# Windowed attention and an MLP-mixer on one core: two opening channel products cut in halves, and the opening's loads and operations in another written order

## The chip, the cores and the metric

The kernel runs on one core of one Trainium2 chip. The metric is device time in microseconds for one execution. The engines named below are TensorE (PE in the profile), VectorE (DVE), ScalarE (ACT), GpSimd (POOL) and SyncE (SP, used here only to issue transfers).

## The reference

Inputs are q, k, v of shape 4 batches x 8 heads x 768 positions x 64, and four mixer weights. Per batch and head, attention is kept to the first 4 keys (the sinks) and to the last 128 keys of each query:

```
scores = scale * np.matmul(q, k.transpose(0, 1, 3, 2))
keep = is_sink | in_window            # key < 4, or 0 <= query - key < 128
a = softmax(np.where(keep, scores, -1e9))
x = (a @ v), heads side by side       # 768 x 512 for each batch
h = np.maximum(xt @ w_tok1, 0.0) @ w_tok2      # xt: x with positions last
u = x + h.transpose(0, 2, 1)
out = u + np.maximum(u @ w_ch1, 0.0) @ w_ch2   # 512 -> 1536 -> 512
```

## The kernel before

**Tiling.** The 32 heads are taken in 8 groups of 4; a batch is two groups (0 and 1, then 2 and 3, and so on). q and k of a group are loaded, cast to bf16 and turned by 32 x 32 blocks on DVE. Scores are made with keys on the partitions, so their exponential is already the transposed operand of the product with v. Key blocks are handled in three pairs (0, 1, 2). The mixer of a batch follows its two groups; its channel part takes the 768 positions in two halves of 384.

**Operations by name.** The kernel builds a list of small operations and names each:

- `Lq0.1` loads piece 1 of q of group 0 (L359 on SP for groups 0 and 1, L371 on POOL for later ones), `Lv` loads v (L381, SP), `Cq`, `Ck`, `Cv` cast, `Tq`, `Tk` turn (L403, DVE), `KZ` prepares the sink keys (L427, DVE).
- `SC0.12` is the score product of group 0, key pair 1, heads from 2 on (L448 and L455). In groups 0 and 1 it covers two heads and one bank, later four heads and two banks. `EX` is its exponential (L472, ACT), `MK` the mask multiplication in SBUF (L483, DVE), `SK` and `EXK` the same for the sinks (L509 PE, L514 ACT).
- `PV0.3` is the product with v for query block 3 of group 0 (L528, L531, L536), `XB0.3` its division by the row sum into `x_b` (L551, L552, DVE).
- `T1b.` is the first token product of batch b (L580), `H1b.` its rectifier; `TT` and `UE` make the transposed `uT` directly for the first half of batch 0, one pair for each of four channel blocks (L611 and L614 on PE; the evacuation at L233 or L235); `T2` and `U` make u in the other layout (L632 PE, L637 DVE), `X` and `UTE` transpose it (L642 PE; L233 or L235).
- `C10.03` is the first channel product of batch 0, half 0, block 3 of twelve (L665): four matmuls, one for each channel block of `uT`. `V` is its rectifier (L239 ACT or L241 DVE). `C20.200` is a third of the second channel product of batch 0, position block 2 (L687), `O` adds u (L697, DVE), `ST` stores (L702, SP).

**Order.** `order_of` is a planner: with an estimated duration for each operation it places, one after the other, the operation that can start first, choosing among those that start within 0.2 us by priority. Its result fixes the order of the instructions on every engine; each engine then runs its own list in that order and waits where a producer is late. For the opening the list `FIRST` gives each named operation its priority and its engine (`:P` is PE, `:A` ACT, `:D` DVE, `:G` POOL, `:S` SP). Everything that is not in `FIRST` is placed by the estimates, so it depends on the times which the planner expects for what stands ahead. `Filler` puts matmuls on zeros (`warm`, L800) where the planner expects PE to be idle in the first 29 us, at the start above all.

**PSUM.** Eight banks: two pairs called "sc" for scores (and for the paired `PV` of group 1) and four single banks called "mx" for everything else. A bank is taken by the first matmul of an operation and given back by the operation that reads it out (`XB` for a `PV`, `V` for a C1, `O` for a whole C2, `UTE` for an `X`). The planner also writes down which bank each operation takes.

**Staging.** The stage pool has four buffers for loaded v (and q, k of group 1). `behind_of` makes the load of `w_tok1` wait for v of group 0, and loads of v of groups 2 and 3 for the last part of `w_ch1`. In the emission order both before and after, `Lv0.0` stands ahead of `Lv1.0` and `Lv1.1`.

Of the kernel before, what the change touches and what calls it, by code (L numbers as in the profile page):

```python
# [9 lines left out]
FP32 = mybir.dt.float32  # L10
# [6 lines left out]


FIRST = """
warm:D blk:G Lq0.0:S kz:D vsink:A Lk0.0:S ones:D va:G Lq0.1:S zero:D first:G Lk0.1:S Lq1.0:S mneg:G first1:D  # L20
Lk1.0:S Lv0.0:S Lv1.0:S rest:G mnegs:D Cq0.0:A Lv1.1:S ident:G Tq0.0:D vs1:G Ck0.0:A vsl:G Tk0.0:D Cq0.1:A
Tq0.1:D Ck0.1:A Tk0.1:D KZ0:D SC0.22:P Cq1.0:G SC0.10:P EX0.21:A SC0.02:P EX0.10:A Tq1.0:D Ck1.0:G EX0.01:A
SC0.00:P SC0.12:P Tk1.0:D EX0.00:A SK0:P EX0.11:A Wtok1:G SC0.20:P Cv0:D EX0.20:A SC1.02:P Wtok2:G EXK0:A
SC1.10:P MK0.20:D Wch1.0:G EX1.01:A PV0.1:P PV0.3:P XB0.1:D Wch1.1:G PV0.5:P EX1.10:A KZ1:D SC1.20:P XB0.5:D
Wch1.2:G XB0.3:D SC1.00:P EX1.20:A Cv1:G PV0.0:P PV0.2:P XB0.0:D EX1.00:A SC1.12:P XB0.2:D Wch1.3:G SK1:P
EX1.11:A MK1.0256:D SC1.22:P Wch2.0:G MK1.00:D EXK1:A T10.000:P MK1.10:D Wch2.1:G PV1.0:P EX1.21:A PV1.1:P
T10.010:P PV0.4:P XB1.0:D PV1.2:P PV1.3:P XB0.4:D PV1.4:P XB1.2:D PV1.5:P T10.004:P XB1.4:D T10.014:P H10.00:A
T10.100:P H10.01:A T10.110:P T10.104:P T10.114:P H10.10:D TT0.00:P H10.11:A TT0.01:P UE0.00:A TT0.03:P
UE0.01:A TT0.02:P UE0.03:A UE0.02:A C10.03:P C10.02:P V0.03:A C10.00:P V0.02:A C10.01:P V0.00:A V0.01:D
"""  # L30


# [125 lines left out]
def kernel(  # L158
# [13 lines left out]
    nc = tc.nc  # L172
    B, H, S, D = q.shape
    P = 128
# [4 lines left out]
    NC = DM // P  # L179
# [5 lines left out]
    HS = S // 2  # L185
# [141 lines left out]
    groups = [Group() for _ in range(NG)]  # L327
# [236 lines left out]
    def mixer(b, base, mbase):  # L564
        M = batches[b]
# [4 lines left out]
        for a in range(GB):  # L570
            for tt in range(NTOK):
                p = Psum("mx", 1)

                xs, o, cut = groups[GB * b + a].xb, None, [0, 4, 6] if b == 0 else [0, 6]
                for lo, hi in zip(cut, cut[1:]):
                    def tok1(e, a=a, tt=tt, p=p, lo=lo, hi=hi):
                        if lo == 0:
                            open_psum(p, [P, W], FP32, "ps_h")
                        for t in range(lo, hi):
                            nc.tensor.matmul(p.tile, w_tok1[:, t, ts(tt, P)], xb.tile[:, t, ds(a * W, W)],  # L580
                                             start=(t == 0), stop=(t == NT - 1))
                    o = op(f"T1{b}.{a}{tt}{lo}", ("PE", 0.11 * (hi - lo)), tok1,
                           xs[:hi * len(xs) // NT] + [w_ops["tok1"], o], base, take=[p] if lo == 0 else [])
# [19 lines left out]
        if direct:  # L603
            for hf in range(NDIR):
                for c in range(NC):
                    p = Psum("mx", 1)
# [10 lines left out]
                    def evac(e, hf=hf, c=c, p=p):  # L617
                        copy_on[e](uT_of(hf)[:, c], p.tile)
                    a = c * P // W
                    o = op(f"TT{b}.{hf}{c}", ("PE", 0.5), tok2t,  # L620
                           M.h1[NTOK * a:NTOK * a + NTOK] + groups[GB * b + a].xb + [w_ops["tok2"]], base + 1 if hf == 0 else mbase + 0.2, take=[p])
# [4 lines left out]
        for st in range(NT):  # L626
            p, p2 = Psum("mx", 1), Psum("mx", 1)
# [19 lines left out]
            o = op(f"T2{b}.{st}", ("PE", 0.431), tok2, M.h1 + [w_ops["tok2"]], later, take=[p])  # L647
# [11 lines left out]
        def c1(hf, ft, pri):  # L659
            p = Psum("mx", 1)  # L660

            def emit(e):
                ps = open_psum(p, [P, HS], FP32, "ps_v")
                for c in range(NC):
                    nc.tensor.matmul(ps, w_ch1[:, c, ts(ft, P)], M.uT[hf][:, c], start=(c == 0), stop=(c == NC - 1))  # L665
            o = op(f"C1{b}.{hf}{ft}", ("PE", 0.652), emit,
                   M.ready[hf] + [w_ops["ch1", ft // 3]], pri, take=[p])
            M.c1.append(o)

            def relu(e):  # L670
                if M.v1t[hf] is None:
                    M.v1t[hf] = vpool.tile([P, NF, HS], BF16, name=f"v1{hf}")
                relu_on(e, M.v1t[hf][:, ft], p.tile)
            old = prev.c2[hf] if prev else []
            M.v1[hf].append(op(f"V{b}.{hf}{ft}", {"ACT": act(HS), "DVE": dve(HS)}, relu, [o] + old, pri - 5, free=[p]))
# [43 lines left out]
    w_ops = {}  # L719
# [29 lines left out]
        w_ops[key].follows = list(w_ops.values())[-2:-1]  # L749
        return w_ops[key]  # L750

    spq = [o for g in (0, 1) for o in groups[g].plain] + groups[0].load["v"] + groups[1].load["v"]
    for x, y in zip(spq, spq[1:]):
        y.follows = y.follows + [x]

    weight("tok1", w_tok1, moe_w_tok1.rearrange("(t p) n -> p t n", p=P), [groups[0].load["v"][0]], -40, 60)
    weight("tok2", w_tok2, moe_w_tok2.rearrange("(t p) n -> p t n", p=P), [], -39, 135)
    qf = DCH // 4
# [10 lines left out]
    for b in range(B):  # L769
        batches[b].x = X(batches[b - 2].u if b >= 2 else [])  # L770
        for a in range(GB):
            g = GB * b + a
# [9 lines left out]
    for n, word in enumerate(FIRST.split()):  # L782
        name, e = word.split(":")
        e = {"P": "PE", "A": "ACT", "D": "DVE", "G": "POOL", "S": "SP"}[e]
        o = by_name[name]
# [53 lines left out]
```

The softmax here doesn't subtract the row's maximum and nothing guards it: scores larger than these inputs give would overflow.

## Time and profile before

| | us |
|---|---|
| median of 6 runs | 215.89 (215.64 to 216.06) |
| the profiled execution, its own time | 215.94 |
| its span in the trace | 214.2 |
| PE busy | 205.3 (96%) |
| DVE busy | 126.4 (59%) |
| ACT busy | 108.2 (50%) |
| first score matmul starts | 11.16 |
| first channel matmul (L665) starts | 31.38 |

The time of an execution is 1.74 us more than the span: that part lies outside the first and last instruction. Matmuls overlap in their pipeline, so PE counts as busy also where it only just keeps up; a share of 96% over the span says nothing of one stage. The granted TensorE clock is full in all forty slices. The DMA engines are busy for nine tenths or more of the slices from about 5 to 75 us.

### The profile page before, as it was taken

How to read it: one execution, taken by the hardware profiler on the slowest of the kernel's cores; microseconds unless marked ns; L12 is line 12 of the kernel's file. 1: busy time of each engine (PE TensorE's matmuls, PEld its weight loads, DVE VectorE, ACT ScalarE, POOL GpSimd, SP SyncE). 2: the span in 40 equal slices, each digit the busy share in tenths (PEclk: the TensorE clock that was granted, in tenths of full speed). 3: DMA queues.
4: the chain of work that ended last, by engine and by line, in shares of the span. 5: the costliest groups of instructions: out<-in, count | busy, mean ns of one | idle time of the engine just before them, and what ended most of it. 6: DMA issues, size and time to landing. Idle time of an engine off the chain costs nothing.

```text
span 214.2 us, 4175 instructions
## 1 busy us (share of the span) xinstructions
PE 205.3 (96%) x1764; PEld 116.2 (54%) x1764; DVE 126.4 (59%) x224; ACT 108.2 (50%) x178; POOL 33.2 (15%) x54
## 2 busy tenths in 40 slices
PE   7999999999689999989999999999999999999993
PEld 2435776554356655466655544667555545655552
DVE  4786941598799989898998812786621122001121
ACT  7478556533847133989518520796553302743300
POOL 7739710002352200110000000000000000000000
PEclk9999999999999999999999999999999999999999
DMA  6999999999999982950001012100001122001122
GB/s 201 381 223 164 203 205 204 206 212 232 219 222 238 250 189 79 180 92 0 3 0 52 0 68 110 71 0 3 0 3 49 49 98 98 3 2 49 49 101 99
DMA packets 36244, 24.68 MB, mean 115 GB/s; under 512 B 26112, under 2 KB 30976, under 8 KB 36224
## 3 DMA queue, kind: packets, MB, share of 16 engines
q1 hardware_dynamic: 29184, 15.73, 28.8%
q0 software_dynamic: 7040, 8.67, 24.1%
q8 instruction: 14, 0.23, 0.4%
q14 instruction: 6, 0.05, 0.1%
HBM read 26.77 MB, written 6.29 MB: 154 GB/s over the span
## 4 chain that ended last, share of the span: by engine, by line
PE 91%; DVE 4%; ACT 2%; issue 1%; ACTq 0%
PE ps_w L687 29%; PE ps_v L665 28%; PE ps_s L455 7%; PE ps_h L580 5%; PE ps_warm L800 5%; PE ps_u L632 5%; PE ps_o L531 3%; DVE pT L483 2%; PE ps_o L528 2%; PE ps_o L536 2%; PE ps_ut L642 2%; ACT pT L472 2%; PE ps_k L509 1%; PE ps_s L448 1%; DVE x_b L552 1%
## 5 line engine op out<-in xcount | busy, mean ns | idle before, releaser
L665 PE MATMUL ps_v<-uT,w_ch 128*128 128x384 bf16 x384 | 67.9, 326 | 0.0
L239 ACT ACTIVATE v<-ps_v 128x384 bf16<-128x384 f32 x89 | 43.4, 493 | 48.5 <-PE ps_v L665 37.4
L687 PE MATMUL ps_w<-w_ch,v 128*128 128x512 bf16 (+1 forms) x300 | 66.1, 371 | 0.0
L472 ACT ACTIVATE pT<-ps_s 128x1024 bf16<-128x1024 f32 (+1 forms) x48 | 43.7, 954 | 13.9 <-PE ps_s L455 10.1
L665 PEld LDWEIGHTS <-w_ch 128*128 128x128 bf16 x384 | 36.5, 98 | 25.3 <-DVE x_b L552 0.4
L697 DVE TENSOR_TENSOR o<-ps_w,u_sb 128x512 f32<-128x512 f32 (+1 forms) x25 | 16.7, 669 | 55.9 <-PE ps_w L687 55.8
L687 PEld LDWEIGHTS <-v 128*128 128x128 bf16 x300 | 28.9, 98 | 29.6 <-issue 0.2
L483 DVE TENSOR_TENSOR pT<-pT,mrest 128x1536 bf16<-128x1536 bf16 (+2 forms) x21 | 20.8, 990 | 2.6 <-ACT pT L472 2.5
L637 DVE TENSOR_TENSOR u_sb<-ps_u,x_b 128x512 bf16<-128x512 f32 x24 | 15.2, 683 | 10.1 <-PE ps_u L632 10.1
L552 DVE TENSOR_TENSOR x_b<-ps_o,rc 128x256 bf16<-128x256 f32 (+1 forms) x45 | 19.9, 442 | 1.6
L455 PE MATMUL ps_s<-qT,kT 32*128 32x256 bf16 (+1 forms) x384 | 18.2, 263 | 1.0 <-ACT pT L472 1.0
L403 DVE STREAM_TRANSPOSE qT<-qb 128x768 uint32<-128x768 uint32 (+1 forms) x9 | 16.8, 1867 | 2.7 <-POOL qb L234 1.4
L531 PE MATMUL ps_o<-va,pT 128*128 128x65 bf16 x192 | 16.2, 194 | 1.0 <-DVE o L697 0.8
L403 DVE STREAM_TRANSPOSE kT<-kb 128x768 uint32<-128x768 uint32 (+1 forms) x9 | 16.9, 1874 | 0.4 <-POOL kb L234 0.4
L234 POOL CAST va<-raw_v 128x1536 bf16<-128x1536 f32 x7 | 10.3, 1477 | 41.6 <-DMA raw_v<-in_v_dram 24.5
L455 PEld LDWEIGHTS <-kT 32*128 32x128 bf16 x384 | 9.8, 92 | 11.2 <-issue 9.0
L531 PEld LDWEIGHTS <-pT 128*128 128x128 bf16 x192 | 13.5, 98 | 2.7 <-DVE o L697 1.2
L536 PE MATMUL ps_o<-va,pT 128*128 128x65 bf16 x160 | 14.8, 193 | 0.0
L632 PE MATMUL ps_u<-h,w_tok 128*128 128x512 bf16 x48 | 12.6, 378 | 0.6 <-ACT uT L235 0.5
L580 PE MATMUL ps_h<-x_b,w_tok 128*128 128x256 bf16 x96 | 12.2, 273 | 0.0
L800 PE MATMUL ps_warm<-warm 128*128 128x512 bf16 (+1 forms) x36 | 10.7, 464 | 1.3 <-DVE warm L255 1.3
L536 PEld LDWEIGHTS <-pT 128*128 128x128 bf16 x160 | 11.3, 98 | 0.8 <-issue 0.3
(63 smaller groups left out, 135.3 us busy)
## 6 DMA issues: line engine op xcount, KB each, us to landing
out_dram<-o SPq DMA_DIRECT2D x23, 256.0 KB, 2.0
raw_v<-in_v_dram SPq DMA_DIRECT2D x7, 768.0 KB, 12.3
qb<-in_q_dram POOLq DMA_DIRECT2D x6, 384.0 KB, 8.5
kb<-in_k_dram POOLq DMA_DIRECT2D x6, 384.0 KB, 12.4
w_ch<-in_moe_w_ch_dram POOLq DMA_DIRECT2D x4, 384.0 KB, 9.9
w_ch<-in_moe_w_ch_dram POOLq DMA_DIRECT2D x1, 1024.0 KB, 15.2
raw_q<-in_q_dram SPq DMA_DIRECT2D x2, 384.0 KB, 4.3
raw_k<-in_k_dram SPq DMA_DIRECT2D x2, 384.0 KB, 4.8
```

The lines of the kernel that those rows point to most:

```text
L239: nc.scalar.activation(o, i, AF.Relu)
L403: nc.vector.transpose(G.T[w].rearrange("p s x -> p (s x)").bitcast(UINT32).rearrange("p (i r) -> p r i", i=Q)[:, r], G.bf[w][:, r].bitcast ...
L455: nc.tensor.matmul(bank[h][:, at:at + w], G.T["k"][r, ts(kt, P), db], G.T["q"][r, ds(kt * P, w), db], start=not pem and db == 0, stop=db = ...
L472: nc.scalar.activation(o, i, AF.Exp, scale=scale)
L483: nc.vector.tensor_tensor(out=t, in0=t, op=ALU.mult, in1=m[:, 0:hi - lo].rearrange("p (o x) -> p o x", o=1).to_broadcast([P, GH, hi - lo]))
L531: nc.tensor.matmul(ps[:, h], G.pT[qt // 2][:, h, ds(256 * (qt % 2), P)], G.va[:, h, qt], start=(qt < 2 and h == 0), stop=(h == GH - 1 and ...
L536: nc.tensor.matmul(ps[:, h], G.pT[kt // 2][:, h, ds(256 * (kt % 2) + P, P)], G.va[:, h, kt], start=False, stop=(h == GH - 1), skip_group_c ...
L552: nc.vector.tensor_tensor(out=xb.tile[:, ds(q0, n), c0:c0 + W].rearrange("p n (h d) -> p n h d", h=GH), in0=ps[:, :, :, 0:D], in1=rc.to_br ...
L580: nc.tensor.matmul(p.tile, w_tok1[:, t, ts(tt, P)], xb.tile[:, t, ds(a * W, W)], start=(t == 0), stop=(t == NT - 1))
L632: nc.tensor.matmul(ps, w_tok2[:, tt, ts(st, P)], M.h1t[:, tt], start=(tt == 0), stop=(tt == NTOK - 1))
L665: nc.tensor.matmul(ps, w_ch1[:, c, ts(ft, P)], M.uT[hf][:, c], start=(c == 0), stop=(c == NC - 1))
L687: nc.tensor.matmul(p.tile, M.v1t[hf][:, ft, ts(st % NH, P)], w_ch2[:, ft, ds(lo, n)], start=(ft == 0), stop=(ft == NF - 1))
```

## The change

Three edits are made.

1. `FIRST` is rewritten. On SP the four quarter loads of group 0 come in the order k1, q1, q0, k0 in place of q0, k0, q1, k1. The cast of that first k piece goes from ACT to DVE, the cast of q of group 1 from POOL to DVE. On POOL the mask constants are built in another order (`blk` later). On PE the twelve score products of groups 0 and 1, and with them exponentials, masks and products with v, are listed in another order; `T20.3` and `T20.4`, which ran ahead of the first channel products because the planner placed them there, are no longer there; `UE0.02`, `V0.02` and `V0.00` go to DVE.
2. In `c1`, the first four blocks of half 0 of batch 0 are two operations each of two matmuls: `C10.00a` on channel blocks 0 and 1, `C10.00` on 2 and 3. Each half waits only for its own two blocks of `uT`; the second half adds into the same bank.
3. The planner's extra rule that placed the loads on SP one after the other in a given order (`spq`) is taken out. It adds no instruction and no wait of its own to the program.

```diff
-warm:D blk:G Lq0.0:S kz:D vsink:A Lk0.0:S ones:D va:G Lq0.1:S zero:D first:G Lk0.1:S Lq1.0:S mneg:G first1:D
...
+warm:D kz:D va:G Lk0.1:S Lq0.1:S ones:D ident:G vsink:A Lq0.0:S zero:D rest:G Lk0.0:S first:G Lq1.0:S Lk1.0:S
+mneg:G first1:D Lv0.0:S Lv1.0:S Ck0.1:D Lv1.1:S blk:G mnegs:D Tk0.1:D vs1:G Cq0.1:A vsl:G Tq0.1:D Cq0.0:A
+Tq0.0:D Ck0.0:A Tk0.0:D KZ0:D SC0.22:P Cq1.0:D SC0.02:P EX0.21:A Tq1.0:D SC0.12:P EX0.01:A Ck1.0:G SK0:P
...
+T10.100:P T10.110:P H10.00:D T10.104:P T10.114:P H10.10:A TT0.00:P H10.11:A TT0.01:P UE0.00:A TT0.02:P
+UE0.01:A TT0.03:P UE0.02:D C10.00a:P UE0.03:A C10.02a:P C10.02:P C10.00:P V0.02:D C10.03a:P C10.03:P V0.00:D
+C10.01a:P V0.03:A C10.01:P V0.01:A
...
-            def emit(e):
-                ps = open_psum(p, [P, HS], FP32, "ps_v")
-                for c in range(NC):
-                    nc.tensor.matmul(ps, w_ch1[:, c, ts(ft, P)], M.uT[hf][:, c], start=(c == 0), stop=(c == NC - 1))
-            o = op(f"C1{b}.{hf}{ft}", ("PE", 0.652), emit,
-                   M.ready[hf] + [w_ops["ch1", ft // 3]], pri, take=[p])
+            o = None
+            for lo, hi in ((0, NC // 2), (NC // 2, NC)) if b == hf == 0 and ft < 4 else ((0, NC),):
+                def emit(e, lo=lo, hi=hi):
+                    if lo == 0:
+                        open_psum(p, [P, HS], FP32, "ps_v")
+                    for c in range(lo, hi):
+                        nc.tensor.matmul(p.tile, w_ch1[:, c, ts(ft, P)], M.uT[hf][:, c], start=(c == 0), stop=(c == NC - 1))
+                o = op(f"C1{b}.{hf}{ft}" + ("" if hi == NC else "a"), ("PE", 0.163 * (hi - lo)), emit,
+                       (M.ready[hf][lo:hi] if b == hf == 0 else M.ready[hf]) + [w_ops["ch1", ft // 3], o], pri, take=[p] if lo == 0 else [])
...
-    spq = [o for g in (0, 1) for o in groups[g].plain] + groups[0].load["v"] + groups[1].load["v"]
-    for x, y in zip(spq, spq[1:]):
-        y.follows = y.follows + [x]
```

More of the change, by code (lines that the diff above doesn't have):

```diff
@@ L19 @@
 FIRST = """
-warm:D blk:G Lq0.0:S kz:D vsink:A Lk0.0:S ones:D va:G Lq0.1:S zero:D first:G Lk0.1:S Lq1.0:S mneg:G first1:D
[L21 to L29, printed above, removed]
+warm:D kz:D va:G Lk0.1:S Lq0.1:S ones:D ident:G vsink:A Lq0.0:S zero:D rest:G Lk0.0:S first:G Lq1.0:S Lk1.0:S
+mneg:G first1:D Lv0.0:S Lv1.0:S Ck0.1:D Lv1.1:S blk:G mnegs:D Tk0.1:D vs1:G Cq0.1:A vsl:G Tq0.1:D Cq0.0:A
+Tq0.0:D Ck0.0:A Tk0.0:D KZ0:D SC0.22:P Cq1.0:D SC0.02:P EX0.21:A Tq1.0:D SC0.12:P EX0.01:A Ck1.0:G SK0:P
+EX0.11:A SC0.20:P EX0.20:A SC0.10:P Tk1.0:D EXK0:A SC0.00:P EX0.10:A Wtok1:G KZ1:D EX0.00:A SC1.22:P Cv0:D
+Wtok2:G MK0.20:D SC1.10:P Wch1.0:G EX1.21:A PV0.0:P PV0.1:P EX1.10:A Wch1.1:G XB0.0:D PV0.2:P PV0.5:P XB0.1:D
+Cv1:G SC1.02:P XB0.2:D SC1.00:P EX1.01:A XB0.5:D PV0.4:P Wch1.2:G PV0.3:P XB0.4:D EX1.00:A SC1.12:P Wch1.3:G
+XB0.3:D SK1:P EX1.11:A MK1.00:D SC1.20:P Wch2.0:G MK1.0256:D EXK1:A Wch2.1:G T10.010:P MK1.10:D EX1.20:A
+T10.014:P PV1.0:P PV1.1:P T10.000:P H10.01:A XB1.0:D PV1.2:P PV1.3:P PV1.4:P XB1.2:D PV1.5:P T10.004:P XB1.4:D
+T10.100:P T10.110:P H10.00:D T10.104:P T10.114:P H10.10:A TT0.00:P H10.11:A TT0.01:P UE0.00:A TT0.02:P
+UE0.01:A TT0.03:P UE0.02:D C10.00a:P UE0.03:A C10.02a:P C10.02:P C10.00:P V0.02:D C10.03a:P C10.03:P V0.00:D
+C10.01a:P V0.03:A C10.01:P V0.01:A
 """
```

## The prediction

> **What bounds the kernel now.** I read the busy line and the chain first (PE holds 91% of it), then the table of stretches, since a mean of 96% hides where PE waits.
>
> ```profile
> PE 205.3 (96%) x1764; PEld 116.2 (54%) x1764; DVE 126.4 (59%) x224; ACT 108.2 (50%) x178; POOL 33.2 (15%) x54
> ```
>
> ```profile
> core 0: us, PE busy (x) PEld busy (x) DVE busy (x) ACT busy (x) POOL busy (x), PEclk, DMA share, GB/s
> 0.00:11.20 11.20, 9.94 (x34) 3.82 (x36) 6.42 (x13) 6.69 (x7) 8.66 (x26) 1.00 0.83 288
> 11.20:20.00 8.80, 8.78 (x107) 4.31 (x106) 6.86 (x8) 7.71 (x9) 5.35 (x7) 1.00 1.26 194
> ...
> 40.00:52.80 12.80, 12.80 (x78) 6.59 (x78) 12.46 (x12) 4.52 (x9) 1.47 (x1) 1.00 1.12 220
> 52.80:64.00 11.20, 9.03 (x119) 4.81 (x119) 8.93 (x17) 7.28 (x10) 5.00 (x6) 1.00 1.32 220
> 64.00:76.00 12.00, 11.98 (x148) 7.79 (x147) 11.35 (x26) 5.64 (x8) 2.94 (x2) 1.00 1.11 239
> ...
> 88.00:102.00 14.00, 12.76 (x198) 8.22 (x197) 12.25 (x29) 12.67 (x20) 2.00 (x2) 1.00 0.43 84
> ...
> 118.00:134.50 16.50, 16.50 (x83) 7.96 (x82) 6.54 (x10) 3.86 (x7) 0.00 (x0) 1.00 0.17 64
> ```
>
> Three regimes. Until 52.8 us PE has no hole after its first instruction; until 11.2 it runs only filler. From 52.8 to 118 DVE is nearly as full as PE and PE has holes. From 118 us PE is full to the end. The instruction lists of PE, ACT and DVE from `SK6` (134.3 us) on are the same in both kernels, so the change is worth what it moves `SK6`.
>
> PE over the opening:
>
> ```profile
> 1.26 9.96 PE L800 MATMUL ps_warm<-warm 128*128 128x512 bf16 x32 [1.26 <-DVE warm L255]
> ...
> 9.69 0.24 DVE L427 TENSOR_TENSOR kz<-kT,blk 128x32 bf16<-128x32 bf16 x1
> ...
> 11.16 0.51 PE L455 MATMUL ps_s<-qT,kT 32*128 32x256 bf16 x8
> ```
>
> The last turn of k ends before KZ, at about 9.9 us; the first score waits for the filler.
>
> The middle, PE's two longest holes, then DVE's work:
>
> ```profile
> 58.17 0.30 PE L531 MATMUL ps_o<-va,pT 128*128 128x65 bf16 x4 [0.83 <-DVE o L697]
> 61.66 0.28 PE L528 MATMUL ps_o<-vsink,pk 128*128 128x260 bf16 x1 [0.56 <-DVE x_b L552]
> ```
>
> ```profile
> 59.06 1.99 DVE L483 TENSOR_TENSOR pT<-pT,mrest 128x2048 bf16<-128x2048 bf16 x1
> ...
> 67.59 0.42 DVE L241 TENSOR_SCALAR h<-ps_h 128x256 bf16<-128x256 f32 x1
> 68.32 1.23 DVE L483 TENSOR_TENSOR pT<-pT,mrest 128x2048 bf16<-128x2048 bf16 x1 [0.31 <-ACT pT L472]
> ...
> 73.76 0.68 DVE L697 TENSOR_TENSOR o<-ps_w,u_sb 128x512 f32<-128x512 f32 x1
> 74.35 2.07 DVE L403 STREAM_TRANSPOSE qT<-qb 128x768 uint32<-128x768 uint32 x1
> ...
> 82.47 2.07 DVE L403 STREAM_TRANSPOSE kT<-kb 128x768 uint32<-128x768 uint32 x1
> ```
>
> PE waits here for PSUM banks that DVE has not read out, and DVE is a queue: whatever stands in it ahead of an `XB` delays the next product with v.
>
> **The Trainium skill.** "Perfetto Trace Analysis", section Identifying Performance Opportunities, says that a repeated gap on the engine that should be full can mean too few PSUM buffers; the two holes above, both ended by a DVE read-out, agree. "SBUF — State Buffer", section Who interferes with whom: a `tensor_tensor` with both inputs in SBUF and a GpSimd operation that reads SBUF exclude each other for the whole instruction. The mask at 59.06 agrees: 1.99 us against 1.23 for the same form at 68.32, with POOL's cast of v running from 58.51 for 1.47 us. That cast waits for a transfer, so this stall doesn't move with the opening.
>
> **The change, part by part.** Nothing outside `FIRST` is ordered by hand, so the change also reorders the middle: I read both programs' lists. Below, each engine's list is walked in its own order with durations of the trace of before: start to start, a C1 takes 0.65 us, a C2 third 0.86, T2 0.43, X 0.22, a PV 0.36; on DVE a turn 1.97 (2.07 less overlap), a mask 0.60, 1.13 or 0.86 by size, an XB 0.55, an O or U 0.60, a V 0.46. The same walk of before's lists lies at most 0.4 us from its trace up to 84 us and under 1.1 at 118; I use differences of the two walks.
>
> *Loads.* SP issues the same transfers; arrivals stay at about 4.3, 5.2, 6.9 and 7.9 us, only now k1, q1, q0, k0. The last two still need a cast (0.84) and a turn (about 1.0) each: 7.9+0.84, and behind the other turn, gives 9.9 us again. The first cast on DVE (at most 0.96, the price of the twice larger v cast; delayed up to 0.6 if POOL's mask building holds it off) ends by 5.8, its turn and q1's by 7.8, just when q0 is cast: hidden. The POOL constants move within time in which nothing waits. v's order is as before: zero.
>
> *Filler.* 30 instead of 32 at the start. Spacing: (3.55-0.10)/16 = 0.216 us over the loads of the later ones. Gain 0.43; both filler pairs later remain.
>
> *Casting q of group 1 on DVE*: its turn starts about 10.9 instead of 11.30, but k's still waits for arrival and POOL's cast to 13.7. Zero.
>
> *Halved channel products.* PE had no wait to lose: `T20.3` and `T20.4` (0.86) covered the last evacuations. After the change halves cover them and both T2 come after the twelfth C1: -0.86+0.86. New small waits: 0.10 for `UE0.03`; 0.08 before `X0.3` (one T2 less between it and its add) and 0.20 for the bank of `UTE0.3` (0.39+0.60 and two hand-overs of 0.05 against 0.87 of PE work); one mask and two bank waits in 23-27 us are about 0.1 more than before. `C20.000` comes before `C10.10`: no sum changes. Net at `SC2.00`: -0.43+0.1+0.1+0.28 = about -0.1 with rounding. The turns of groups 2 and 3 (from 43.13 us) and POOL's casts of v (51.18 and 54.90) start when transfers land, so DVE gains nothing from an earlier PE here.
>
> *From 55 to 75.* DVE now has `MK2.10` ahead of `XB2.0`. `PV2.2` waits for that bank to the same 61.6 us, but before, `C20.200` (0.86) ran in the hole; now it stands behind `PV2.5`: +0.9. Then `Tq4.0` moves from 74.35 to between `H11.00` and `MK3.10`. q of group 4 landed 7.5 us after issue at 59.92, so at 67.4, just in time. The turn begins at about 67.7 and `MK3.10` at 69.6 instead of 68.3: +1.3. Behind it come `XB3.0`, `MK3.20` and now `XB3.1` after it. Two of the four single banks are held by `C20.2` and `C20.3`, whose adds now stand after `XB3.5` on DVE, so the last PV take turns in two banks: `XB3.1` ends at 72.8, `PV3.3` 72.9, `PV3.4` 73.4, `PV3.5` 74.1, `C20.400` at 74.7 against 72.8. In walks, 74.7-72.4; with the opening's -0.1 inside, `C20.400` is late by +2.2, minus that 0.1.
>
> *After 75.* Gains: `Tk4.0` is at 76.4 instead of 82.5, so `SC4.00` fills PE between the X: waits of 0.6 vanish. `EX4` starts at 81 instead of 86, and of 2.0 us waits at `SC4.20` to `PV4.3` only about 1.1 stay (`PV4.2` still stands 0.75 for the bank of `V1.00`, behind `EX4.21` on ACT): -0.9. Losses: `Tk5.0` (86.9 before) comes after `XB4.5`, at 93.8, so scores and exponentials of group 5 are late; waits at `PV5.0`, `SC5.20`, `PV5.3`, `PV5.4`, `T12.100` make 1.3 against 0.7: +0.6. `Tk7.0` (118.64 before) stands ahead of `U2.0`, and `X2.1`, `X2.2`, `T22.3` wait 1.15 against 0.57: +0.6.
>
> Sum: -0.1+2.2-0.6-0.9+0.6+0.6 = +1.8; I take 1.7, since the walk's waits are rounded upward by hand-overs. The profiled execution would go from 215.94 to 217.6 (span 215.9). It stands 0.05 above the median, which I neglect: 217.6.
>
> The unknown costs: if q of group 4 lands 0.5 us earlier or 1 us later (v of group 7 may be issued earlier and share the engines), the turn costs nothing less, since DVE is not free before 67.7, and up to 1 more. DVE's own port waits: from -0.3 to +0.3. Misjudged waits in 75-118, which the walk of before missed by 0.7 there: from -1 to +1.
>
> **Rivals.**
>
> A. *Faster.* The turns are only moved, so what 67-75 loses comes back in full: `Tk4.0` and `Tq4.0` done early empty the DVE queue before group 4, both its waits (2.0 and 0.6) vanish, group 5 and batch 2 lose nothing. Then +2.1-2.6-0.0 and the opening's 0.43 kept whole: -0.9, 215.0. It decides if `SK6` comes before 134.2. For it: DVE's total is unchanged. Against: ACT is 12.67 of 14 us busy in 88-102, so exponentials, not only turns, set that stretch.
>
> B. *No change*: later gains equal the loss, 215.9. It needs the losses of group 5 and batch 2 (1.2) to be absent and 0.5 more.
>
> C. *Slower than forecast.* q of group 4 arrives a us later and DVE stands before `Tq4.0` with everything behind it: +1, 218.6. For it: the DMA engines are full until 75 us. Against: it is first of its four transfers.
>
> D. *The halves don't help because evacuations are late*: ACT has `UE0.00`, `UE0.01`, `UE0.03` at 0.49 each; if PE stood for all four it would be 0.4, inside the range.
>
> **Chances.** Forecast (216.6 to 218.2) 0.59, A 0.13, B 0.07, C and worse 0.21. Within 0.2% is 215.46 to 216.32, about what a measurement of this kernel can tell from no change. Faster 0.12 (A, nearly all), same 0.08, slower 0.80. The range cuts off most of A and the far end of C: 215.7 to 219.0; the likeliest case's own is 216.6 to 218.2.
>
> **What would show it.** First score at about 10.75 us; `SC2.00` within 0.4 of 52.7. On DVE a turn of qT near 67.7, right after the rectifier of h; `C20.400`, the first L687 matmul after the last product with v of group 3, near 74.7 or later. A turn of kT before the first u add of batch 2, near 110. A PE hole below 1.2 us around 88-93. PE full from about 120. The prediction is wrong if `SC2.00` comes before 52 us and stays early, or if PE's holes between 75 and 118 sum to less than 2 us.

## The result, and the profile after

| | before | after |
|---|---|---|
| median, us | 215.92 (72 runs) | 216.89 (35 runs, 216.45 to 218.71) |
| ratio | | 1.0061, 95% interval 1.0047 to 1.0075 |
| the profiled execution, us | 215.94 | 216.67 |
| its span, us | 214.2 | 215.0 |
| `SC0.22`, first score | 11.16 | 10.02 |
| `SC2.00`, first score of group 2 | 52.78 | 51.78 |
| `C20.400`, the C2 third behind group 3 | 72.80 | 74.36 |
| `C21.000`, first C2 of batch 1 | 106.36 | 106.59 |
| `C21.100` | 118.74 | 119.49 |
| `SK6`, from where both programs are alike | 134.29 | 135.04 |

The change makes the kernel slower, by 0.6% as the ratio has it and by 0.45% (0.97 us) by the medians. The forecast was 0.8%, and the median lies inside its range. Eight of the 35 executions of after show a mean granted clock of 0.992 and took 217.9 to 218.7 us, while the other 27 took 216.45 to 217.30, and the ratio, which is of means, keeps these eight. The 0.75 us at `SK6` are all of the 0.73 by which the profiled executions differ. They are made of a gain of 1.0 us in the opening, a loss that turns it into +1.56 at `C20.400`, a recovery of 1.33 by `C21.000`, and a second loss of 0.52.

The busy line of after:

```profile
PE 204.4 (95%) x1762; PEld 115.7 (54%) x1762; DVE 129.9 (60%) x227; ACT 107.2 (50%) x176; POOL 32.5 (15%) x53
```

The stretches of after, with the same borders as those shown of before; the columns are the stretch, its length, the busy time of each engine with its instructions, the granted clock and the DMA share:

```profile
core 0: us, PE busy (x) PEld busy (x) DVE busy (x) ACT busy (x) POOL busy (x), PEclk, DMA share, GB/s
0.00:11.20 11.20, 9.71 (x44) 3.92 (x46) 8.61 (x16) 6.46 (x7) 7.53 (x25) 1.00 0.83 287
...
40.00:52.80 12.80, 12.80 (x85) 6.71 (x84) 11.56 (x10) 4.87 (x11) 1.47 (x1) 1.00 1.11 219
52.80:64.00 11.20, 8.75 (x118) 4.92 (x117) 9.91 (x21) 8.40 (x11) 6.46 (x7) 1.00 1.34 220
64.00:76.00 12.00, 10.55 (x122) 6.26 (x120) 10.27 (x21) 3.73 (x5) 2.46 (x3) 1.00 1.12 231
88.00:102.00 14.00, 13.41 (x151) 8.15 (x150) 13.75 (x19) 11.12 (x21) 2.52 (x3) 1.00 0.36 57
118.00:134.50 16.50, 16.50 (x85) 8.13 (x83) 5.58 (x9) 4.68 (x9) 0.00 (x0) 1.00 0.20 72
```

In these stretches PE stands (does no work) for 2.45 us in 52.8 to 64 and for 1.45 in 64 to 76, where it stood 2.17 and 0.02 before. In 88 to 102 it stands for 0.59 instead of 1.24, and DVE is full there (13.75 of 14.00). From 118 us PE is full, as before.

The opening on PE, filler and the first score:

```profile
1.26 8.54 PE L800 MATMUL ps_warm<-warm 128*128 128x512 bf16 x30 [1.26 <-DVE warm L256]
10.02 0.51 PE L456 MATMUL ps_s<-qT,kT 32*128 32x256 bf16 x8 [0.22 <-DVE kT L404]
```

The filler takes 8.54 us in place of 9.96 and so ends 1.42 us earlier, so far that the score now waits 0.22 us for the turn of k.

DVE in the middle (start, length, instruction; in brackets how long the engine stood and for what), first of before, then of after:

```profile
55.49 1.42 DVE L483 TENSOR_TENSOR pT<-pT,mfirst 128x1024 bf16<-128x1024 bf16 x1 [0.27 <-ACT pT L472]
56.83 0.68 DVE L483 TENSOR_TENSOR pT<-pT,mrest 128x1024 bf16<-128x1024 bf16 x1
57.43 0.68 DVE L697 TENSOR_TENSOR o<-ps_w,u_sb 128x512 f32<-128x512 f32 x1
```

```profile
54.48 0.69 DVE L484 TENSOR_TENSOR pT<-pT,mfirst 128x1024 bf16<-128x1024 bf16 x1 [0.27 <-ACT pT L473]
55.09 1.96 DVE L484 TENSOR_TENSOR pT<-pT,mrest 128x1024 bf16<-128x1024 bf16 x1
...
58.03 1.21 DVE L484 TENSOR_TENSOR pT<-pT,mrest 128x2048 bf16<-128x2048 bf16 x1
...
65.80 0.42 DVE L242 TENSOR_SCALAR h<-ps_h 128x256 bf16<-128x256 f32 x1 [0.20 <-PE ps_h L581]
67.39 2.09 DVE L404 STREAM_TRANSPOSE qT<-qb 128x768 uint32<-128x768 uint32 x1 [1.16 <-DMA qb<-in_q_dram]
69.27 1.26 DVE L484 TENSOR_TENSOR pT<-pT,mrest 128x2048 bf16<-128x2048 bf16 x1
...
76.14 2.08 DVE L404 STREAM_TRANSPOSE kT<-kb 128x768 uint32<-128x768 uint32 x1
```

POOL at the same time, the casts of v of groups 3 and 4 (before, then after), and in after the load of q of group 4:

```profile
54.90 1.47 POOL L234 CAST va<-raw_v 128x1536 bf16<-128x1536 f32 x1 [2.24 <-DMA raw_v<-in_v_dram]
58.51 1.47 POOL L234 CAST va<-raw_v 128x1536 bf16<-128x1536 f32 x1 [2.14 <-PE ps_o L531]
```

```profile
55.03 1.47 POOL L235 CAST va<-raw_v 128x1536 bf16<-128x1536 f32 x1 [2.24 <-PE ps_s L456]
58.65 1.92 POOL L235 CAST va<-raw_v 128x1536 bf16<-128x1536 f32 x1 [2.15 <-PE ps_s L456]
60.52 1.05 POOL L372 DMA_DIRECT2D qb<-in_q_dram  x2
```

And PE's waits there:

```profile
57.70 0.30 PE L532 MATMUL ps_o<-va,pT 128*128 128x65 bf16 x4 [1.37 <-DVE o L701]
...
72.55 0.28 PE L529 MATMUL ps_o<-vsink,pk 128*128 128x260 bf16 x1 [0.89 <-DVE x_b L553]
```

Read together: in before the first mask of group 2 runs behind the cast that begins at 54.90 and takes 1.42 us, 0.74 more than its neighbour. In after it passes ahead (54.48), but the second mask comes 0.06 us behind the cast that begins at 55.03, and takes 1.96 us instead of 0.68. So the add at 56.97, for which PE waits 1.37 us, is only 0.46 us earlier than before, of the 1.0 that the opening had gained. The next mask is ahead of the next cast: now the mask takes 1.21 us (1.99 before) and the cast 1.92 (1.47 before).

The load of q of group 4 is issued on POOL behind that cast, at 60.52 (59.92 before), and lands at 67.36. The later issue is not what holds it: in before it landed at 67.40. In both profiles it lands 1.6 us after v of group 6 (65.77 and 65.75). What is new is that something waits for it. DVE is ready at 66.2 and stands 1.16 us, because the order puts the turn of q ahead of the mask at 69.27. PE then waits for the divisions that are queued behind. The chain of the page, which was PE for 91% and named no transfer among its engines, is now PE 81%, DMA 6% (half of it this load), DVE 5%.

### The profile page after: what moved, and what is told of

The parts are those of the page before. It is cut to its first block, busy times and chain, and to the rows that moved or that the text cites. A ratio compares the mean times of both kernels' runs of the same rounds, so it can differ in the third digit from the quotient of the medians.

```text
span 215.0 us, 4170 instructions
## 1 busy us (share of the span) xinstructions
PE 204.4 (95%) x1762; PEld 115.7 (54%) x1762; DVE 129.9 (60%) x227; ACT 107.2 (50%) x176; POOL 32.5 (15%) x53
## 4 chain that ended last, share of the span: by engine, by line
PE 81%; DMA 6%; DVE 5%; ACT 4%; issue 1%; SPq 1%; POOLq 0%; POOL 0%; ACTq 0%
PE ps_v L669 27%; PE ps_w L691 27%; PE ps_s L456 6%; PE ps_u L633 5%; PE ps_h L581 4%; ACT pT L473 3%; DMA qb<-in_q_dram 3%; DMA raw_k<-in_k_dram 3%; PE ps_o L532 2%; PE ps_ut L643 2%; DVE pT L484 2%; PE ps_o L529 2%; PE ps_o L537 2%; PE ps_k L510 1%; PE ps_s L449 1%
## 5 line engine op out<-in xcount | busy, mean ns | idle before, releaser
L240 ACT ACTIVATE v<-ps_v 128x384 bf16<-128x384 f32 x87 | 42.3, 493 | 45.9 <-PE ps_v L669 35.0
L484 DVE TENSOR_TENSOR pT<-pT,mrest 128x1536 bf16<-128x1536 bf16 (+2 forms) x21 | 21.3, 1021 | 1.6 <-ACT pT L473 1.6
L236 ACT ACTIVATE uT<-ps_ut 128x512 bf16<-128x512 bf16 (+1 forms) x14 | 8.0, 574 | 9.2 <-PE ps_ut L643 8.6
```

What stands on the lines that cost most here:

```text
L240: nc.scalar.activation(o, i, AF.Relu)
L484: nc.vector.tensor_tensor(out=t, in0=t, op=ALU.mult, in1=m[:, 0:hi - lo].rearrange("p (o x) -> p o x", o=1).to_broadcast([P, GH, hi - lo]))
```

## Experiments

In all these kernels the order of every engine is written out as a list which the planner follows. Left as they are, the lists give the order of the kernel before or after exactly, so that a part of one can be put beside a part of the other. "Opening" is everything up to `T20.2` on PE and `U0.2` on DVE. The reference point in each set is the kernel before, timed between them (216.07 us in the first set, 215.98 in the others); the sets ran on different chips, so a difference between kernels of two sets is good to about 0.1 us. The "old rest" and the "new rest" are the orders of before and after behind a border. Where a kernel of this section has a diff of a list, only the edited stretch is shown.

### Opening alone, middle alone

```diff
 lists of the kernel after up to T20.2 (PE), UTE0.4 (ACT), U0.2 (DVE), Lv1.1 (SP)
-the rest of the kernel after
+the rest of the kernel before
```

> The opening of the changed kernel up to the last u of batch 0 (T20.2 on PE, U0.2 on DVE), and behind it the order of the kernel before on every engine, for the rest. Theory (the loss lies in the reordered middle, the opening itself gains): the opening's 0.4 to 1.0 us is kept in good part, so 215.0 to 215.7 us, below the kernel before; no turn of q of group 4 before the masks of group 3, waits of PE from 75 to 118 us as before (about 3.5 us). Rival 1 (the opening gains nothing that lasts, since turns and casts of groups 2 and 3 start when transfers land): 215.9. Rival 2 (the new opening is what costs): 216.5 to 217.

Measured: 216.20 us, ratio 1.0008 (0.9990 to 1.0027). That is nearest to the rival by which nothing of the opening's gain lasts: the new opening alone is worth nothing that can be measured, although it brings `SC2.00` forward (52.51 in this profile, whose granted clock is half in 60.2 to 63.6 us; hence all later starts of its row in a table below are about a microsecond late).

```diff
 lists of the kernel before up to T20.2, UTE0.3, U0.2, Lv1.1
-the rest of the kernel before
+the rest of the kernel after
```

> The reverse: the opening of the kernel before, whole channel products and all, and behind it the order of the changed kernel. Theory: the whole loss of the middle without the opening's gain, 217.2 to 218.2 us. Rival 1: the same as the changed kernel, 216.9. Rival 2 (the opening costs): 215.9, as before.

Measured: 216.67 us, ratio 1.0028 (1.0008 to 1.0048). It is less than either theory that expected a loss had, and not the 215.9 of a costly opening. So the loss comes from the reordered middle: +0.6 to +0.75 us with either opening (216.89 against 216.20, and 216.67 against 215.92 to 216.07). `C20.400` is at 74.72 us here, the forecast's 74.7.

### The halves alone

```diff
-TT0.00 TT0.01 TT0.03 TT0.02 T20.3 T20.4 C10.03 C10.02 C10.00 C10.01 ...
+TT0.00 TT0.01 TT0.02 TT0.03 C10.00a C10.02a C10.02 C10.00 C10.03a C10.03 C10.01a C10.01 ... T20.3 T20.4
```

> The kernel before with only the halved channel products: from the first TT to the last u of batch 0 the order of the changed kernel (halves, the two T2 behind the twelfth product, UE0.02 on DVE), everything ahead and behind as in the kernel before. Theory (the two T2 covered the evacuations already): 215.8 to 216.2 us, no difference or a little slower by the 0.3 us of new waits. Rival (the halves are worth the 0.86 us of PE time ahead of the first channel product): 215.0 to 215.3.

Measured: 216.23 us, ratio 1.0016 (0.9998 to 1.0035). The edit cuts four products in two (`C10.00` to `C10.03`, where the title says two; only the halves of `C10.00` have others between them). From the first score to `SC2.00` it takes 42.07 us against 41.62 or 41.63 in before and in four more profiles with the old opening: the halves give no gain and cost up to 0.45, as one would expect if the evacuations were already covered by `T20.3` and `T20.4`. The time doesn't tell it from no change.

### The turn of q of group 4 put late

```diff
-H11.00 Tq4.0 MK3.10 XB3.0 ... XB3.5 O0.20 O0.30 Tk4.0
+H11.00 MK3.10 XB3.0 ... XB3.5 O0.20 O0.30 Tq4.0 Tk4.0
```

> The changed kernel with one operation moved: the turn of q of group 4 stands on DVE behind the add of position block 3 (O0.30), where the kernel before has it, and no longer ahead of the second mask of group 3. Theory (that turn, and DVE standing 1.2 us for its transfer, delays the products with v of group 3): the last product of group 3 starts 1.5 to 2.5 us earlier than 73.8, and part of it is lost again because the turn of k of group 4 comes 2 us later; 215.9 to 216.5 us. Rival (DVE has the same work either way, so only the place of the wait moves): 216.7 to 217.0.

Measured: 217.33 us, ratio 1.0053 (1.0040 to 1.0067): not faster than after. The theory that the early place of this turn makes the loss fell. DVE and POOL of this kernel, then PE:

```profile
55.09 0.69 DVE L525 TENSOR_TENSOR pT<-pT,mrest 128x1024 bf16<-128x1024 bf16 x1
55.12 1.98 POOL L276 CAST va<-raw_v 128x1536 bf16<-128x1536 f32 x1 [2.24 <-PE ps_s L497]
...
66.58 1.23 DVE L525 TENSOR_TENSOR pT<-pT,mrest 128x2048 bf16<-128x2048 bf16 x1 [0.79 <-ACT pT L514]
...
74.47 2.08 DVE L445 STREAM_TRANSPOSE qT<-qb 128x768 uint32<-128x768 uint32 x1
76.34 2.12 DVE L445 STREAM_TRANSPOSE kT<-kb 128x768 uint32<-128x768 uint32 x1
78.25 1.92 DVE L679 TENSOR_TENSOR u_sb<-ps_u,x_b 128x512 bf16<-128x512 f32 x3
```

```profile
72.73 1.04 PE L732 MATMUL ps_w<-w_ch,v 128*128 128x512 bf16 x4
...
79.03 0.40 PE L684 MATMUL ps_ut<-ident,u_sb 128*128 128x128 bf16 x4 [0.94 <-DVE u_sb L679]
79.63 0.40 PE L684 MATMUL ps_ut<-ident,u_sb 128*128 128x128 bf16 x4 [0.20 <-DVE u_sb L679]
79.96 0.63 PE L497 MATMUL ps_s<-qT,kT 32*128 32x256 bf16 x16
```

The mask is at 66.58 and `C20.400` at 72.73, 1.63 us earlier than in after. But now both turns stand in a row ahead of the u adds, PE waits 0.94 and 0.20 us for these, and from the score at 79.96 on it is only 0.15 us ahead of after (80.11). The turn of k is reached at 76.34 us here and at 76.14 in after.

This profile differs from after in a second thing: the second mask of group 2 starts 0.03 us ahead of the cast of v of group 3, takes 0.69 us, and the cast takes 1.98. So the 1.63 us are not the price of the turn's place alone; the next section has the late turn without this. The profiled execution took 216.53 us and is the shortest of its 22 runs. That the mask falls behind the cast in the longer ones would fit a median 0.8 above it, but no trace shows one.

### The border moved to 75 us

```diff
 lists of the kernel before up to PV3.5 (PE), EX3.21 (ACT), O0.30 (DVE)
-the rest of the kernel before
+the rest of the kernel after, Tq4.0 first on DVE
```

> The order of the kernel before up to the last product with v of group 3 (PV3.5 on PE, O0.30 on DVE), and the changed order only behind it, the turn of q of group 4 directly behind O0.30. Theory as put before the chip (the loss is made by 75 us, group 5 and batch 2 cost 1.2 us, gains of 1.5 us lie in 75 to 94): C20.400 at 72.8 us as in the kernel before, and the end about 0.3 us earlier than it, 215.6 to 215.9 us. New theory (in the changed order PE may not pass SC4.00, which stands ahead of the rest of batch 1 and needs both turns of group 4, so the place of one turn is nothing by itself): SC4.00 near 80 us as in the changed kernel whatever C20.400 does, and the same end as with the whole changed middle, 216.5 to 216.9.

Measured: 216.45 us, ratio 1.0026 (1.0013 to 1.0040): slower than before, where the theory from the forecast had it faster, and just under the band of the new one.

```diff
 lists of the kernel before up to T20.2, then of the kernel after up to PV3.5, EX3.21, O0.30
-the rest of the kernel after
+the rest of the kernel before
```

> The reverse: opening of the kernel before, changed order from there to PV3.5 and O0.30 (so with the early turn of q of group 4), and behind it the order of the kernel before. Theory as put before the chip: C20.400 1.9 us late (74.7) and little comes back, since before has only 0.6 us of waits there that an earlier turn could take away: 217.0 to 217.8 us. New theory: late at C20.400 too, and nothing of the 2.0 us that DVE has done ahead is of use to PE, since SC4.00 stands late in PE's list: the same, 217.3 to 217.8. A rival that blames group 5 and batch 2 alone: 215.9 to 216.3.

Measured: 217.60 us, ratio 1.0092 (1.0058 to 1.0126). By medians the changed stretch up to 75 us alone costs about twice what the whole middle costs (1.62 us, from six runs), and the changed rest alone has its cost too (0.47 us). So the two do not add: together they cost less than the first alone. Start times in the profiles show why (us):

| kernel | turn of q4 | `C20.400` | turn of k4 | `C11.00` | `SK6` |
|---|---|---|---|---|---|
| before | 74.35 | 72.80 | 82.47 | 83.88 | 134.29 |
| opening alone | 75.40 | 73.84 | 83.51 | 84.92 | 135.32 |
| new to 75 | 67.74 | 74.75 | 84.41 | 85.82 | 137.70 |
| after | 67.39 | 74.36 | 76.14 | 86.98 | 135.04 |
| middle alone | 67.75 | 74.72 | 76.49 | 87.33 | 135.39 |
| turn of q4 late | 74.47 | 72.73 | 76.34 | 86.83 | 134.88 |
| new from 75 | 74.47 | 72.92 | 76.34 | 86.82 | 134.88 |

In the old rest, PE carries the lateness of `C20.400` on: `C11.00` comes 11.07 or 11.08 us behind it in all three kernels (the third also fell to a granted clock of 0.88 and 0.93 in 90 to 110 us, so its last column and part of its time are not the order's doing).

In the new rest two bounds lie close together. In after, and in "middle alone", `C11.00` comes 12.61 or 12.62 us behind `C20.400`, and PE doesn't wait once in between. In the last two kernels it comes 14.1 and 13.9 us behind it, and 10.48 or 10.49 behind the turn of k: there PE waits for the u adds that DVE does after this turn. PE and DVE in 75 to 82 us (and 82 to 90), of after, then of "turn of q4 late" (columns as in the stretches above):

```profile
75.00:82.00 7.00, 7.00 (x62) 4.13 (x61) 6.71 (x11) 2.53 (x5) 1.47 (x2) 1.00 0.94 232
82.00:90.00 8.00, 8.00 (x88) 4.49 (x87) 7.31 (x14) 5.46 (x8) 0.05 (x1) 1.00 0.21 73
```

```profile
75.00:82.00 7.00, 5.86 (x49) 2.78 (x48) 7.00 (x10) 2.31 (x4) 2.46 (x3) 1.00 0.97 211
```

So `C11.00` is at the later of `C20.400` + 12.61 and the turn of k + 10.48. This gives its time within 0.01 us in all seven kernels with the new rest, those of the sections below among them. In after the two are 86.97 and 86.62. `C20.400` alone could thus have come earlier by 1.6 us and the end by no more than 0.35; it takes an earlier turn of k as well. In the four kernels of the table with the new rest `SK6` follows `C11.00` by 48.05 or 48.06 us.

### The add that frees a bank, put earlier

```diff
-MK3.10 XB3.0 MK3.20 XB3.1 ... XB3.5 O0.20 O0.30 Tk4.0
+MK3.10 XB3.0 O0.20 MK3.20 XB3.1 ... XB3.5 O0.30 Tk4.0
```

> The changed kernel with the add of the third output block (it frees a PSUM bank) moved on DVE from behind the last XB of group 3 to right behind its first. Theory W (the forecast's two-bank step: the last products with v take turns in two banks and so the next C2 third is late): the next C2 third begins at 73.6 to 74.0 instead of 74.4 and the end follows, 216.4 to 216.6. Rival V (DVE is full up to the turn of k of group 4, whose start near 76.2 no exchange ahead of it moves, and PE waits for what stands behind): the third may be earlier, that turn stays within 0.2 of 76.1, time 216.8 to 217.0.

Measured: 216.66 us, ratio 1.0044 (1.0026 to 1.0062), between the two theories' bands. The trace decides. DVE of this kernel:

```profile
67.48 2.09 DVE L445 STREAM_TRANSPOSE qT<-qb 128x768 uint32<-128x768 uint32 x1 [0.99 <-DMA qb<-in_q_dram]
...
71.09 0.68 DVE L742 TENSOR_TENSOR o<-ps_w,u_sb 128x512 f32<-128x512 f32 x1
...
75.88 2.07 DVE L445 STREAM_TRANSPOSE kT<-kb 128x768 uint32<-128x768 uint32 x1
```

The bank is free at 71.8 us instead of 75.5, and `C20.400` begins at 74.33 against 74.36. DVE shows no hole from the turn of q up to the turn of k at 75.88, so the add only changes places with a mask and divisions that come 0.7 us later, and the last products with v wait for these as before. An exchange within DVE's queue doesn't help PE here. Whether more banks without such an exchange would, no run tells. `SK6` is at 135.00.

### The casts of v on ACT

The kernel before, with the casts of v of groups 3 and 4 taken from POOL to ACT (behind the exponentials of the sinks of group 3 and the last of group 2). The load of q of group 4, which stood behind them on POOL, is made to wait for the load of v of group 4 instead:

```diff
         veng = {"POOL": 0.96e-3 * N}
+        if g in (3, 4):
+            veng["ACT"] = act(N)
...
-                    nc.gpsimd.dma_start(out=bf(), in_=src)
+                    ins = nc.gpsimd.dma_start(out=bf(), in_=src)
+                    if g == 4 and w == "q":
+                        behind_of(ins, groups[4].load["v"][0])
```

> The kernel before with the casts of v of groups 3 and 4 on ACT (behind EXK3 and EX2.21) in place of POOL; the first load behind them on POOL is made to wait for v of group 4, so that the transfers stay in order. Theory (POOL's casts, timed by landing transfers, hold off DVE's masks at 55 and 59 us, 0.74 and 0.77 us): those masks take 0.69 and 1.2 us, SC3.00 comes 0.8 to 1.4 us earlier, and 0.3 to 1.0 us of it reach the end: 214.9 to 215.6 us. Rival (the masks are long for another reason): the same 1.4 and 2.0 us, and 215.9 or more, since ACT has 3.1 us of work more.

Measured: 214.49 us over six runs, ratio 0.9933 (0.9914 to 0.9953), below the band of the theory; the rival fell. The profiled execution is the slowest of the six (215.02 us), and its `SK6` is 0.93 us earlier than in before. The same edit on "opening alone":

> The same two casts on ACT, in the kernel with the opening of the changed kernel and the middle of the kernel before. Theory (what the opening gains is lost in front of the same casts and landings): without them the gain of 0.3 to 1.0 us at SC2.00 lasts beyond 62 us, and the end is 0.3 to 0.8 us earlier than with the old opening and the casts on ACT: 214.3 to 215.1 us. Rival (the opening's gain is lost elsewhere): no difference from the old opening with the casts on ACT.

Measured: 214.14 us over six runs, ratio 0.9918 (0.9895 to 0.9940), a little under the theory's band. It is faster than both before and after. Its masks of group 2 on DVE:

```profile
54.91 0.69 DVE L529 TENSOR_TENSOR pT<-pT,mfirst 128x1024 bf16<-128x1024 bf16 x1 [0.27 <-ACT pT L518]
55.52 0.68 DVE L529 TENSOR_TENSOR pT<-pT,mrest 128x1024 bf16<-128x1024 bf16 x1
...
57.83 1.22 DVE L529 TENSOR_TENSOR pT<-pT,mrest 128x2048 bf16<-128x2048 bf16 x1
```

None is held up. The 0.53 us by which its `SC2.00` is ahead of the other's (52.20 against 52.73) is 0.59 at `C20.400` (71.29 against 71.88) and 0.60 at `SK6` (132.76 against 133.36); the medians differ by 0.35, which the intervals alone would not tell from nothing. By the starts in the profiles, with the casts away a gain of the opening goes through.

The same edit on the whole kernel after:

> The changed kernel with the casts of v of groups 3 and 4 on ACT instead of POOL. Theory P (q of group 4 and the early turns hold the middle: DVE is free sooner but stands for that transfer at about 67 us, and behind it the two turns bind up to 83 us): time 216.0 to 216.5, and 1.9 us or more above the same casts with the old middle (214.1). Rival Q (the casts alone took what the new opening gains, the new middle costs its 0.5 to 0.7 us again): masks of group 2 near 0.6 and 1.2 us, time 214.6 to 215.0.

Measured: 215.60 us, ratio 0.9990 (0.9971 to 1.0010), 1.29 below after and 1.46 above the kernel just before, which has the same opening and casts and the old middle. Neither theory had it. POOL and DVE of this kernel:

```profile
59.34 1.05 POOL L413 DMA_DIRECT2D qb<-in_q_dram  x2 [6.25 <-DVE rc L597]
```

```profile
65.98 0.42 DVE L283 TENSOR_SCALAR h<-ps_h 128x256 bf16<-128x256 f32 x1 [0.36 <-PE ps_h L626]
66.33 2.07 DVE L447 STREAM_TRANSPOSE qT<-qb 128x768 uint32<-128x768 uint32 x1
...
75.08 2.07 DVE L447 STREAM_TRANSPOSE kT<-kb 128x768 uint32<-128x768 uint32 x1
```

The edit took away more than the first theory allowed for: q lands at 65.97 instead of 67.36, and so before DVE comes to it. The load is issued at 59.34 instead of 60.52, but the transfers have also changed places. In eleven profiles, all those with these casts on POOL, q of group 4 lands 1.59 to 1.65 us after v of group 6, wherever between 59.88 and 61.18 its issue is. In the three with the casts on ACT its issue begins before SP has finished issuing v of group 6 (59.34 and 59.50 here), and it lands 7.4 to 7.9 us ahead of v of group 6. Whether the overlap of the issues decides this is not shown.

The turn starts 1.06 us earlier than in after, and all that follows is earlier by that much (`C20.400` by 1.02, `SK6` by 1.04). By these starts the wait for this transfer is the link between the opening and the end in the kernel after. What is left, 1.46 us by medians (1.24 at `SK6`), is the price of the new middle where these casts are on ACT.

### The turn of k of group 7 put late

```diff
-KZ6 Tq7.0 Tk7.0 U2.0 ... MK6.00 MK6.0256 KZ7 MK6.10
+KZ6 Tq7.0 U2.0 ... MK6.00 MK6.0256 Tk7.0 KZ7 MK6.10
```

> The changed kernel with one DVE instruction moved: the turn of k of group 7 goes back behind the first masks of group 6, where the kernel before has it. Theory L (the forecast's last step: standing ahead of the first u add of batch 2 it costs 0.6 us): that add starts near 109.8 instead of 111.4, the last C2 of batch 1 begins 0.5 to 0.8 us earlier, time 216.2 to 216.4. Rival M (PE in 110 to 118 us is bound by its own work and by ACT, and the turn only delays the masks of group 6 instead): 216.8 to 217.0, no change against the changed kernel.

Measured: 216.29 us, ratio 1.0021 (1.0004 to 1.0038), 0.6 below after. DVE:

```profile
108.47 2.08 DVE L445 STREAM_TRANSPOSE qT<-qb 128x768 uint32<-128x768 uint32 x1
111.08 1.89 DVE L679 TENSOR_TENSOR u_sb<-ps_u,x_b 128x512 bf16<-128x512 f32 x3 [0.54 <-PE ps_u L674]
...
119.72 2.08 DVE L445 STREAM_TRANSPOSE kT<-kb 128x768 uint32<-128x768 uint32 x1
```

From `C21.000` to `C21.100` PE takes 12.32 us instead of 12.90, so the turn's early place cost 0.58, as the first theory had it. (In this profile q of group 4 landed 0.8 us later than in after, and `C20.400` and `C21.000` are 0.84 and 0.83 later for it.) The first u add did not come near 109.8, also with these 0.83 taken off; it is bound by PE's product at 111.08. So 0.58 of the 0.75 us at `SK6` are this turn's place, and without it the new opening and the rest of the new middle together cost 0.17. "New from 75" says the same: its `SK6` is 0.59 later than in before.

### Less filler in the kernel before

```diff
-            n, w = (11 + int((us - 4.8) / 0.216), 512) if first else (round(us / 0.11), 256)
+            n, w = (5 + int((us - 4.8) / 0.216), 512) if first else (round(us / 0.11), 256)
```

> The kernel before with 26 filler matmuls ahead of the first score instead of 32, nothing else. First score near 9.9 us, where the turn of k ends, instead of 11.2; first score of group 2 near 51.6 instead of 52.8. Theory S (the gain is taken back where the casts of v on POOL, which start when their transfers land, shut DVE's masks out): the C2 third behind group 3 begins within 0.4 of 72.8, time 215.6 to 216.0. Rival G (it goes through to the end): 214.6 to 215.0. If filler is needed for the clock, the opening's matmuls run slow and it is 216.5 or more.

Measured: median 215.89 us over 22 runs, from 213.36 to 224.31. Eight runs had a granted clock of 0.946 to 0.967 over the whole and took 219.3 us or more, and the profile is of one of these. The ratio is 0.9933 (0.9910 to 0.9956) over 13 of the others, which spread from 213.4 to 216.2 us, so that it is a mean of unlike executions. PE in the profile:

```profile
1.26 7.31 PE L845 MATMUL ps_warm<-warm 128*128 128x512 bf16 x26 [1.26 <-DVE warm L297]
10.18 0.51 PE L497 MATMUL ps_s<-qT,kT 32*128 32x256 bf16 x8 [1.61 <-DVE kz L469]
...
11.16 1.03 PE L497 MATMUL ps_s<-qT,kT 32*128 32x256 bf16 x8
...
20.18 1.03 PE L497 MATMUL ps_s<-qT,kT 32*128 32x256 bf16 x8
```

The filler ends at 8.57, PE stands 1.61 us for the turn of k, and a microsecond after the scores have begun eight of them take 1.03 us instead of 0.51. The granted clock is half from 11.2 to 24.9 us. Other executions of the same program kept the full clock. Six of these took 213.4 to 213.7 us, less than either theory had, and the theory that the casts of v take an earlier opening back entirely doesn't fit them. Why they gain about 2.3 us where the filler gave at most 1.3, stays open: no trace shows one of them. One candidate is that the first two masks of group 2 then pass ahead of the cast of v of group 3, which after misses by 0.06 us. Six of the 72 runs of the kernel before lie at 213.5 to 214.3, too; none of the 35 of after is below 216.45.

## Why the prediction was right or wrong

**Right in direction, within its range in size, in part by luck: 217.6 us forecast, 216.89 measured.** The change does what the forecast says in the middle, and the sum of 1.7 came out as 1.0 by medians, 0.75 in the profiles. By stages the profiles show -1.0 up to `SC2.00` where the forecast had -0.1, +2.56 from there to `C20.400` where it had +2.2, and -0.81 behind it where it had -0.3. The part of the opening's gain that was lost again at the casts (0.54) keeps the end near. Two of its own sums don't close: the terms listed for `SC2.00` make +0.05 and not -0.1, and 74.7 less 72.4 is 2.3, where 2.1 is carried on. One reading is off as well: the second longest hole of PE in 52.8 to 76 us is not the one at 61.66 but 0.63 us at 55.50, for an exponential on ACT, and after has it too (0.62 at 54.50). The terms:

- *Loads, the cast of q of group 1.* Nothing, as forecast: the last turn of k ends at about 10.0 us (9.9 forecast), and the score now waits 0.22 us for it. The cast of k on DVE takes 1.12 us (at most 0.96 plus up to 0.6 allowed), hidden.
- *Filler, -0.43.* Mis-sized: the first score came 1.14 us earlier. The filler ended 1.42 us earlier, and the score then waited for k. Two instructions fewer are 0.43 at 0.216 us each; the other 0.99 is that 14 of the filler matmuls took about twice as long (mostly 0.427 us from start to start) in the profile of before, and nine in that of after with a tenth in between (0.243). Over the profiles of these kernels the first score lies between 10.71 and 11.16 us with 32 filler matmuls and between 10.02 and 10.53 with 30. The Trainium skill, "TensorE: Matmul & The Clock Gate", section Part 1: The HAM clock gate (the "warmup" mystery), says that the number of slow first matmuls varies between runs of one kernel. The traces, one for each kernel, agree, and a forecast of such an opening needs a few tenths either way for it.
- *Halves, +0.48 with the small waits.* From the first score to `SC2.00` after takes 41.76 us against 41.62, so +0.14; the halves alone +0.45.
- *The opening's gain and DVE.* "DVE gains nothing from an earlier PE here" was half right. Both kernels' casts start when v lands (54.90 and 55.03 us), and of 1.0 us at `SC2.00` 0.46 was left at the first add. The forecast's first condition for being wrong, `SC2.00` before 52 us and staying early, was met in its first part alone. The Trainium skill, "SBUF — State Buffer", section Who interferes with whom, adds that the order of issue decides which engine is blocked. The traces agree in both directions: mask 1.96 and 1.99 us behind a cast, cast 1.92 and 1.98 behind a mask.
- *55 to 75, +2.1.* Measured +1.56, and +1.92 with the old opening. In "new to 75" the walk is met nearly to the tenth: `PV2.2` 61.62 (61.6), turn of q 67.74 (67.7), `C20.400` 74.75 (74.7). In after the mask escapes its cast and `PV2.2` is at 59.85, and then the step's condition for the turn fails: it does not begin because the rectifier of h is done (66.2) but because q has landed (67.36). That is rival C's wait, at the place where the forecast had the turn for another reason, so it cost nothing more than forecast. The forecast's figure for the landing, 67.4, is right. The forecast said that the turn "costs nothing less" if q came earlier; with the casts on ACT it cost 1.06 less.
- *The two banks.* Not shown as a cause: with one of them freed 3.8 us earlier `C20.400` moves by 0.03, since DVE's queue sets those starts in either order.
- *After 75, -0.6 -0.9 +0.6 +0.6.* Measured -0.8 instead of -0.3 (`C20.400` to `SK6`, 60.68 against 61.49 us). The last term is right: 0.58. The loss of group 5 is not there: PE stands 0.12 us in 97 to 110 us after and 0.16 before, although its scores start 2.55 us later (96.38 against 93.83). The walk took every wait that it saw behind a late turn as lost, and PE had other work. By this the forecast's second condition for being wrong is met: PE's holes between 75 and 118 us sum to 1.27 us in after (1.80 before), and it had asked for 2 or more.
- *The sum itself.* The terms are differences of one walk through the whole new order, and may be added there. They are not prices of single edits, as the experiments show: measured from `C20.400`, the new rest is shorter than the old one (61.49 us) only together with the early turn of q (60.68); with that turn late it takes 62.15 and 61.96. There the turn of k of group 4 is the bound, and an earlier `C20.400` leaves the end where it is.

**The rivals.** A (the loss comes back in full) is refuted by `SK6` at 135.04: 1.33 of 1.56 came back, and then the turn of k of group 7 took 0.58. Without that turn's early place the kernel is still at 1.0021. B needed the losses of group 5 and of batch 2 to be absent and half a us more: that of group 5 is absent, that of batch 2 is not. C's wait is real, 1.16 us, its cost isn't added. D doesn't show.

## What to carry to other kernels

When an edit reorders two stretches, ask for each which queue sets its end. Where two queues come within tenths of each other, as PE's and DVE's do here, moving one earlier gains only up to the other, and differences measured for one stretch at a time may not be added. The time of an issue is not the time of a landing: here one load landed 1.6 us after another transfer over 1.3 us of issue times, and it cost nothing until the new order put a waiting engine in front of the landing. Before an opening is tuned by tenths, look for a pair of instructions whose order of issue is decided by tenths further on: here moving two casts to an engine that doesn't meet the masks gave 1.5 us by medians and 0.93 at `SK6` in the profile, more than the new opening gave.

## What the runs showed of the hardware

- A mask in SBUF on DVE and a cast on POOL block each other, and hundredths of a microsecond decide which way. A mask that starts 0.06 us behind a cast takes 1.96 us (after), one that starts 0.03 us ahead takes 0.69 and the cast 1.98 ("turn of q4 late"); alone they take 0.68 and 1.47. Moving two casts of 1.47 us from POOL to ACT, where each takes 1.50, gave 0.67% (with the load that had stood behind them freed) in a kernel in which POOL was busy for 15%.
- In the kernel with less filler, a stand of 1.61 us on PE was followed by 13.7 us at half the granted clock in one profile (11.2 to 24.9 us), while other runs of the same program kept the full clock. Single stretches of 3.4 us at half the clock stand in two profiles whose mean is 0.989 and 0.992: 60.2 to 63.6 us in "opening alone", 95.4 to 98.8 in "new to 75".
- In eleven profiles the load of q of group 4 landed 1.59 to 1.65 us after that of v of group 6, with issues from 59.88 to 61.18 us; in three it landed 7.4 to 7.9 us before it, with issues from 58.70 to 59.47.
- With all orders fixed, stretches are repeatable to hundredths of a microsecond: from `C20.400` to `SK6` six kernels with the old rest take 61.47 to 61.49 us.
